# A fixed operation table for a whole attention-and-MLP kernel, in place of a scheduler and hand-written ends

## The chip, the cores and the metric

The kernel runs on one core of one Trainium2 chip. The metric is the device time of one execution in microseconds (us), so lower is better. Most executions of a kernel agree within about 1% here; an execution can fall in a slower state, and verdicts use the other ("fast") ones alone.

Names used below: PE is the tensor engine, DVE the vector engine, ACT the scalar engine, SP the queue that issues most loads. PSUM is the memory that PE writes; a *bank* is used here for 512 fp32 columns of it (the scores' tile in the program is 4 x 512). A *softmax block* is one tile of scores (128 x 2048) with its exponential; there are 68. S is "the score matmuls of a block". PEld in the profile is PE's loading of weights, POOL the fifth engine. An *F tile* is one of the 14 blocks of 128 hidden tokens. AV is "attention-value", the product p @ v. Line numbers such as L219 are those of a helper that records operations.

## The reference, cut to what matters

```python
h = layernorm(x) * (1 + ca) + sa            # x: 2048 x 512; sa, ca, ga, ... = silu(c) @ w_mod
q, k, v = split(h @ wqkv)                   # 32 heads of 16
p = softmax(where(0 <= i - j < 256, q k^T / 4, -1e9))
x = x + ga * ((p @ v) @ wo)
h = layernorm(x) * (1 + cb) + sb
u = gelu(layernorm(h)^T @ w1 + b1)          # a matmul over the 2048 rows; 1792 hidden tokens
x = x + gb * (u @ w2 + b2)^T
```

So there are a start (loads, first norm, first projections), a long middle (sliding-window attention, with the first half of the w1 products as filler), and a tail (last norm, the other half of w1, gelu, w2, stores). w1 contracts over rows: its products with the last rows need the last attention output.

## The kernel before: the parts that the argument touches

The loads are issued first, in the order written, on two queues:

```python
nc.scalar.dma_start(out=c4[:], ...)                                # ACT's queue
for v in (0, 1):
    nc.scalar.dma_start(out=wmod[:, :, v * D : (v + 1) * D], ...)  # 512 KB each
for t in range(4):
    dma.dma_start(out=xres[t][:], ...)                             # SP's queue: x, 128 KB a tile
# ... q, k, v weights, x 4..7, the rest of w_mod, wo, x 8..15 ...
dma.dma_start(out=b1b[:], in_=B_b1.rearrange("(j p) -> p j", p=P)) # last: b1 and b2, element by element
dma.dma_start(out=b2b[:], in_=B_b2.rearrange("(j p) -> p j", p=P))
```

The middle is a list of operations with costs and dependencies. A list scheduler in the program puts them in order before building. All score tiles live in the same four PSUM banks, so S of a block waits for the exponential of the block before:

```python
s = op(f"S{i}", "PE", 0.28, e_s, deps=[k_done[G, g8], q_done[G, g8], masks_built] + prev_exp, ...)
x = op(f"E{i}", "ACT", 1.78, e_e, deps=[s] + e_war, ...)
# in the scheduler: other work may not hold up the next S or the next exponential by more than
S_TOL = 0.1
E_TOL = 0.3
```

The tail is written by hand, after the scheduled part:

```python
def mlp1(fcs, scs):
    for sc in scs:                # rows outside, F tiles inside
        for fc in fcs:
            nc.tensor.matmul(ftiles[fc], lhsT=w1s(sc, fc), rhs=hb[sc][:], ...)
first = list(range(6))
mlp1(first, range(8, NT))         # hb[12..15] are the last norm's
for fc in first:
    gelu(fc)                      # addition, gelu, and a DVE multiplication by the gate
# ... the other 8 F tiles, then 16 output tiles of 14 matmuls each, finish(), store
```

The softmax here doesn't subtract the row's maximum and nothing guards it: scores larger than these inputs give would overflow.

## Time and profile before

321.87 us, median of 3 runs (320.91 to 322.01). The profiled execution has a span of 319.8 us. I cut it at the first and the last scores:

| stage | from, to (us) | length |
|---|---|---|
| start, to the first scores | 0, 17.44 | 17.4 |
| attention, first to last scores | 17.44, 217.43 | 200.0 |
| tail, from the last scores | 217.43, 319.8 | 102.4 |

The head of the profile page of before: span, then busy time and share of the span by engine, with the number of instructions.

```profile
span 319.8 us, 12671 instructions
PE 256.3 (80%) x5884; PEld 148.1 (46%) x5937; DVE 196.0 (61%) x376; ACT 176.5 (55%) x168; POOL 32.5 (10%) x87
```

No engine is full over the whole span: the limit differs by stage. The group of exponentials (busy time, mean ns, then ACT's idle time before them and who ended most of it) and that of the scores on PE show the alternation in the middle:

```profile
L219 ACT ACTIVATE et<-pss 128x2048 bf16<-128x2048 f32 x68 | 127.5, 1875 | 29.6 <-PE pss L219 20.3
L219 PE MATMUL pss<-QT,KT 32*64 32x32 bf16 (+5 forms) x1744 | 34.4, 209 | 22.7 <-ACT et L219 20.9
```

The timeline of before, start: first column the time, second the duration, then engine, operation, tiles; in brackets the idle time of that engine before it and what ended it. `ps_fm` makes the modulation vectors from `wmod`; `h1T` is the normed, transposed input of the projections; `KT` the keys as the scores need them; `pss` the scores.

```profile
7.06 0.59 PE L219 MATMUL ps_fm<-sT,wmod 128*128 128x1 bf16 x16 [0.84 <-DMA wmod<-in_w_mod_dram]
7.92 0.68 DVE L219 BATCH_NORM_STATS2 st<-x 128x6 f32<-128x512 bf16 x1
9.81 0.59 PE L219 MATMUL ps_fm<-sT,wmod 128*128 128x1 bf16 x16 [2.17 <-DMA wmod<-in_w_mod_dram]
...
11.80 1.90 DVE L219 TENSOR_SCALAR h1T<-pt,modFM 128x512 bf16<-128x512 bf16 x4 [0.81 <-PE pt L219]
15.97 1.41 DVE L219 TENSOR_SCALAR KT<-pk,mask_par 128x512 bf16<-128x512 f32 x2 [2.27 <-PE pk L219]
17.44 0.40 PE L219 MATMUL pss<-QT,KT 32*128 32x256 bf16 x8 [0.52 <-DVE KT L219]
```

The timeline of before, first part of the tail:

```profile
217.43 0.40 PE L219 MATMUL pss<-QT,KT 32*128 32x256 bf16 x8 [0.16 <-ACT et L219]
...
217.94 1.88 ACT L219 ACTIVATE et<-pss 128x2048 bf16<-128x2048 f32 x1
219.72 0.62 ACT L219 ACTIVATE lz<-lz 128x512 f32<-128x512 f32 x1
...
220.37 0.69 DVE L219 TENSOR_TENSOR OT<-pox,lz 128x512 bf16<-128x512 f32 x1 [2.37 <-ACT lz L219]
222.42 0.70 PE L219 MATMUL pox<-el,VT 128*32 128x32 bf16 x64
...
227.63 0.69 DVE L219 TENSOR_TENSOR x<-pa,x 128x512 bf16<-128x512 f32 x1 [0.50 <-PE pa L219]
...
242.93 1.38 DVE L219 TENSOR_SCALAR hb<-h,mv,rs 128x512 bf16<-128x512 bf16 x4 [0.60 <-ACT rs L219]
243.39 3.57 PE L950 MATMUL pu<-hb,w1p 128*128 128x512 bf16 x8 [9.01 <-DVE hb L219]
...
250.32 1.89 DVE L970 TENSOR_TENSOR a<-pu,part 128x512 f32<-128x512 f32 x3 [6.01 <-PE pu L950]
```

Read: last scores at 217.43, the last attention-value matmuls (`pox`) at +5.0, the first updated x of the last group at +10.2, the last `hb` (input of the MLP) complete at +26.9, first gelu addition 6.0 after that. PE waits 9.01 us for `hb`.

### The profile page before, as it was taken

What the parts mean: (1) busy time and instruction counts of PE and PEld (TensorE: products, weight loads), DVE (VectorE), ACT (ScalarE), POOL (GpSimd) and SP (SyncE); (2) the same over time, 40 slices, a digit from 0 to 9 for tenths busy, and PEclk for the clock granted to TensorE, in tenths of its full rate; (3) what the DMA queues carried; (4) which work ended last, traced back from release to release, by engine and by line L of the source; (5) the groups of instructions that cost most, each with busy time, mean ns of one, the idle gap of its engine ahead of it and who ended that gap; (6) DMA issues with size and microseconds to landing.
All of it is one profiled execution on the core that took longest, in us unless ns stands there. A gap on an engine that the chain in (4) does not pass through costs nothing.

```text
span 319.8 us, 12671 instructions
## 1 busy us (share of the span) xinstructions
PE 256.3 (80%) x5884; PEld 148.1 (46%) x5937; DVE 196.0 (61%) x376; ACT 176.5 (55%) x168; POOL 32.5 (10%) x87
## 2 busy tenths in 40 slices
PE   0678898867897778958888889787935899999973
PEld 0354466444574556624555554544412344444431
DVE  5574988448799746996521669531684667436433
ACT  1168897967887977777787776785102443000000
POOL 8102410130013410003001000000000000000000
PEclk9999999999999999989999999997985999999999
DMA  7993000790000000000201202122002990101100
GB/s 214 338 341 34 3 4 6 201 259 7 5 4 2 4 5 4 4 2 4 70 16 56 70 2 79 58 68 70 3 0 93 412 408 14 60 33 51 49 33 33
DMA packets 31453, 24.94 MB, mean 78 GB/s; under 512 B 6056, under 2 KB 29608, under 8 KB 31400
## 3 DMA queue, kind: packets, MB, share of 16 engines
q1 hardware_dynamic: 30336, 23.08, 23.6%
q10 hardware_dynamic: 1064, 1.05, 1.0%
q8 instruction: 46, 0.75, 0.9%
q14 instruction: 7, 0.06, 0.1%
HBM read 22.03 MB, written 2.10 MB: 75 GB/s over the span
## 4 chain that ended last, share of the span: by engine, by line
PE 46%; ACT 34%; DVE 14%; issue 4%; DMA 1%; POOL 0%; ACTq 0%; DVEq 0%
ACT et L219 30%; PE pu L1004 15%; PE pss L219 10%; PE pu L950 7%; PE pox L219 4%; DVE st L219 3%; PE poy L219 3%; PE pv L219 2%; DVE h L219 2%; PE pk L219 2%; DVE xn L219 1%; ACT rs L219 1%; PE pq L219 1%; ACT lz L219 1%; DVE o L987 1%
## 5 line engine op out<-in xcount | busy, mean ns | idle before, releaser
L219 ACT ACTIVATE et<-pss 128x2048 bf16<-128x2048 f32 x68 | 127.5, 1875 | 29.6 <-PE pss L219 20.3
L219 PE MATMUL pss<-QT,KT 32*64 32x32 bf16 (+5 forms) x1744 | 34.4, 209 | 22.7 <-ACT et L219 20.9
L1004 PE MATMUL pu<-guT,w2r 128*128 128x512 bf16 x220 | 49.3, 379 | 2.8 <-DVE o L987 2.5
L219 PEld LDWEIGHTS <-KT 32*64 32x64 bf16 (+1 forms) x1744 | 24.3, 97 | 39.2 <-issue 35.4
L586 POOL TENSOR_SCALAR KT<-kb,mask_par 128x512 bf16<-128x512 bf16 x30 | 24.5, 827 | 135.4 <-DVE kb L219 75.4
L950 PE MATMUL pu<-hb,w1p 128*128 128x512 bf16 x110 | 28.3, 410 | 11.6 <-DVE hb L219 9.0
L219 PEld LDWEIGHTS <-VT 128*32 128x32 bf16 x1680 | 29.0, 95 | 16.8 <-issue 13.8
L1004 PEld LDWEIGHTS <-w2r 128*128 128x128 bf16 x224 | 21.9, 98 | 29.6 <-issue 3.7
L219 PE MATMUL pox<-et,VT 128*32 128x224 bf16 (+3 forms) x720 | 33.7, 240 | 1.7 <-issue 1.5
L219 PE MATMUL poy<-et,ones_bd 128*32 128x224 bf16 (+3 forms) x720 | 33.0, 237 | 2.1 <-issue 2.1
L987 DVE SCALAR_TENSOR_TENSOR o<-bc_gb,b2FM,pu 128x512 f32<-128x512 bf16 x16 | 11.9, 747 | 25.0 <-PE pu L1004 25.0
L219 PE MATMUL pu<-hb,w1p 128*128 128x512 bf16 x95 | 24.8, 380 | 2.4 <-issue 2.2
L950 PEld LDWEIGHTS <-w1p 128*128 128x128 bf16 x112 | 11.6, 104 | 27.1 <-issue 16.1
L219 DVE COPY part<-pu 128x512 f32<-128x512 f32 x11 | 7.6, 690 | 25.0 <-PE pu L219 25.0
L219 PEld LDWEIGHTS <-ones_bd 128*32 128x32 bf16 x784 | 19.7, 96 | 6.5 <-issue 6.0
L219 DVE BATCH_NORM_STATS2 st<-x 128x6 f32<-128x512 bf16 x32 | 21.7, 679 | 0.2
L219 DVE TENSOR_TENSOR el<-et,maskl 128x2048 bf16<-128x2048 bf16 x16 | 20.0, 1264 | 1.4 <-ACT et L219 1.4
L219 PE MATMUL pq<-h1T,wqkv 128*128 128x512 bf16 x53 | 17.4, 414 | 2.0 <-issue 1.0
L219 DVE TENSOR_TENSOR OT<-pox,lz 128x512 bf16<-128x512 f32 x16 | 11.0, 685 | 12.2 <-ACT lz L219 12.2
L219 PE MATMUL pv<-wqkv,h1T 128*32 128x256 bf16 x512 | 17.1, 273 | 1.6 <-issue 1.6
L219 DVE TENSOR_SCALAR VT<-pv,par_of 128x512 bf16<-128x512 f32 x19 | 13.6, 745 | 7.2 <-PE pv L219 6.0
L219 PEld LDWEIGHTS <-wqkv 128*128 128x128 bf16 x128 | 11.0, 101 | 14.9 <-issue 5.8
(81 smaller groups left out, 306.0 us busy)
## 6 DMA issues: line engine op xcount, KB each, us to landing
w1p<-in_B_w_dram SPq DMA_DIRECT2D x14, 512.0 KB, 4.0
w2r<-in_B_w_dram SPq DMA_DIRECT2D x14, 512.0 KB, 9.3
x<-in_A_x_dram SPq DMA_DIRECT2D x16, 128.0 KB, 5.2
wmod<-in_w_mod_dram SPq DMA_DIRECT2D x4, 512.0 KB, 6.9
out_dram<-otile SPq DMA_DIRECT2D x16, 128.0 KB, 1.7
wmod<-in_w_mod_dram ACTq DMA_DIRECT2D x2, 512.0 KB, 6.2
wqkv<-in_A_wqkv_dram SPq DMA_DIRECT2D x2, 384.0 KB, 7.2
wqkv<-in_A_wqkv_dram SPq DMA_DIRECT2D x1, 512.0 KB, 7.9
```

Of the source, the lines that this page charges most:

```text
L219: ins = call(*args, **kwargs)
L586: eng.tensor_scalar(out=KT[r3][g8][:, :, :, par, :], in0=src[:].rearrange("p (b s k) -> p b s k", s=2, k=HB), scalar1=mask_par[:, par : pa ...
L950: nc.tensor.matmul(ftiles[fc], lhsT=w1s(sc, fc), rhs=hb[sc][:], start=(sc == 8), stop=(sc == NT - 1), skip_group_check=True,)
L987: nc.vector.scalar_tensor_tensor(out=o1[:], in0=bc_gb[:], scalar=b2FM[:, tb : tb + 1], in1=py, op0=ALU.mult, op1=ALU.add,)
L1004: nc.tensor.matmul(ftiles[100 + t], lhsT=w2r[:, fc, t * P : (t + 1) * P], rhs=guT[fc][:], start=(fc == 0), stop=(fc == NF - 1), skip_group ...
```

## The change

Intent: one set of some 1090 numbered operations for everything (loads, attention, both MLP matmuls, stores), cut finer than before, emitted in the order of a table that was searched beforehand, instead of a scheduler for the middle and hand-written ends. The core of the diff (cut):

```diff
-def run_schedule(ops, rings, log=None):      # the list scheduler, about 90 lines
+ORDER = """
+41 30 0 3 42 55 5 49 4 48 13 38 12 54 56 29 1 40 57 78 6 58 2 34 8 37 25 ...
+... 93 19 92A 91D 94 31 24 96D 95A 17 97 98 100 99A 101 104 102A 103D ...
+"""                                          # A or D: on ACT or on DVE
+def run_order(ops):
+    for word in ORDER.split():
+        o = ops[int(word.rstrip("AD"))]
+        o.emit(engines[word[-1]] if word[-1] in engines else next(iter(o.engs)))
+WARM = 24                                    # zero matmuls while PE waits for the first loads
@@ loads become operations of the table @@
-    dma.dma_start(out=b2b[:], ...)           # last
+    o_b = [load("b1", ...), load("b2", ...)] # words 29 and 30
@@ the first transposed input may be copied by either engine @@
-            h = op("h1T", "DVE", 0.95, e_h, deps=[a, o_fm] + before, pos=p_tr)
+                frees.append(op("h1T", {"DVE": 0.45, "ACT": 0.6}, e_h, deps=[tr[1], o_fm] + before, ...))
@@ the tail becomes operations too, F tile by F tile @@
-    mlp1(first, range(8, NT))
+            for lo in range(8, NT, 2):       # two matmuls an operation, in the order of the table
@@ the gate is applied to the result, not to the hidden activations @@
-        nc.vector.tensor_tensor(out=guT[fc][:], in0=g[:], in1=bc_gb[:], op=ALU.mult)
-            in0=bc_gb[:], scalar=b2FM[...], in1=py, op0=ALU.mult, op1=ALU.add
+            in0=ftiles[100 + tb], scalar=b2FM[...], in1=bc_gb[:], op0=ALU.add, op1=ALU.mult
```

In the first words, 0 is c; 1 and 2 the two halves of `wmod`; 3, 4, 5, 6 the first four x tiles; 7 to 28 the other loads (12 and 13 are x tiles of the next group); 29 and 30 are b1 and b2. So b2 now leads SP's queue.

## The prediction

> **What bounds the kernel now** (timeline and chain of waits; span 319.8 us):
> 1. Start: first scores at 17.4 us, after load, statistics, xn, transposes, four h1T copies (1.9 us on DVE), q, k, two KT copies (1.4 us on DVE). The first q and k matmuls are 0.43 us apart, later ones 0.216[...].
> 2. Attention: 17.4 to 217.4 us (last scores), 68 softmax blocks. All score tiles share four PSUM banks, so exponential (1.88 us) and scores (0.53 with hand-over; long form 1.25) alternate: floor 2.44 us, 3.16 for the eight long ones. PE does the rest between. I summed PE's program order between successive scores at measured spacings (512 columns 0.216 us, V projection 0.87, window AV 0.43, local AV 0.73, 0.09 per change of array tiling) and took the larger of sum and floor: 193 us, against 200.0 measured. Some periods are overloaded (up to 7.2 us), others have 1.3 us of work.
> 3. Tail: 102.4 us. The last group's norm chain is serial on DVE (first x at 227.6, last hb about 244); PE waits 9.0 us for hb[...], waits again for the first gelu additions (250.3), then runs back to back; 4.4 us drain.
>
> **What changes.** The matmuls are the same, plus 24 zero ones at the start. It removes 14 DVE multiplies of guT by bc_gb (0.42 us, mostly hidden), splits projections into halves, gives ACT half of the first h1T and KT copies, splits the rs of the first and last group, and fixes the order of everything.
>
> **Costs.**
> - Start: copies shared by ACT and DVE save 0.8 + 0.7 us[...]. Against it: the wmod loads on ACT's queue now follow the exponential that waits for c (3.8 us instead of 1.4), and b2b and b1b lead the SP queue, 3840 two-byte packets that kept the DMA busy about 2.6 us near 25 us. Estimate: first scores at 16.5 us (15.5 to 18.5).
> - Attention: the same count over the new order gives 184 us (largest period 3.6): work is spread evenly. With before's excess of 3.7%, 191.5 (186 to 198), a gain of 8.5. Sixteen partial matmuls (3.5 us) moved into the tail.
> - Tail, from the last scores: AV is no longer held behind w1 matmuls, so the first x comes at about +5.6 us instead of +10.2; the DVE chain still takes 15.8, so hb is complete near +22 instead of +26.6. Meanwhile PE does Wo and half the rows of eight F tiles. Then 288 matmuls remain (62 us) instead of 312, gelu additions follow at once[...], 4.4 drain: +91. Gain 11.5.
>
> Sum: 16.5 + 191.5 + 91 = 299 us span; measured times are some 2 us above the span: **300.5 us**, 8 in 10 between 292 and 310. All of it is on the critical path. Faster by over 2%: 0.94; within 2%: 0.05; slower by over 2%: 0.01.
>
> **What would show it.** First scores at 15.5 to 18.5; first to last scores 186 to 198 us, PE's waits for exponentials and ACT's for scores both smaller; first x of the last group within 7 us of the last scores; PE's wait for hb below 6 us; first gelu addition within 2 us of the last hb; then back-to-back matmuls and the same drain.
>
> **What would make it wrong.** A late x tile, with DVE in order, would hold the first groups: the fixed order may ignore real load arrival. Finer in-order pieces could wait on each other more than 3.7%. [...]

The sum: 16.5 + 191.5 + 91 = 299 us of span, 300.5 us of time. That PE is slower after standing idle, that zero matmuls prevent this, and that a busier PE loses clock was the author's assumption, which no trace shows. Two of these are in the sum: up to 1.3 us of gain in the start's 16.5 (about what six matmuls at 0.43 instead of 0.216 us come to), and 2 us for PE's restart in the tail's +91 (22 + 62 + 2 + 4.4 = 90.4). What the trace of before shows is the spacing: 0.43 us for the first q and k matmuls; and after the 9.01 us wait for `hb` the first eight matmuls took 3.57 us, 0.45 each, at a granted clock of 0.50 (237.1 to 247.3 us), where later ones come every 0.216 us.

## The result, and the profile after

308.87 us median (307.76 to 310.87, 4 runs) against 321.39 of before (4 runs). The ratio is 0.963, 95% interval 0.956 to 0.970: faster. A ratio here is the mean time of one kernel's fast runs over the mean of the other's fast runs of the same rounds, so it is not quite the ratio of the medians quoted.

The time fell inside the range, but only 12.5 us of the forecast 21. By stage, from the two timelines:

| | before | after | forecast for after |
|---|---|---|---|
| first scores at | 17.4 | 21.6 | 16.5 |
| first to last scores | 200.0 | 190.7 | 191.5 |
| last scores to the end | 102.4 | 93.7 | 91 |
| span | 319.8 | 306.0 | 299 |

The attention is as forecast, the tail misses by 2.7 us, and the start **lost** 4.1 us where 0.9 was to be gained. Most of the miss is in the first 22 us. The head of the page of after:

```profile
span 306.0 us, 12754 instructions
PE 263.4 (86%) x5961; PEld 148.4 (49%) x5961; DVE 190.9 (62%) x367; ACT 178.3 (58%) x178; POOL 29.3 (10%) x87
```

The same two groups as before, exponentials and scores:

```profile
L169 ACT ACTIVATE et<-pss 128x2048 bf16<-128x2048 f32 x68 | 127.6, 1876 | 33.3 <-PE pss L169 31.7
L169 PE MATMUL pss<-QT,KT 32*64 32x32 bf16 (+5 forms) x1744 | 35.4, 210 | 14.1 <-ACT et L169 10.1
```

PE's waits for exponentials halved (20.9 to 10.1 us), but ACT's waits for scores grew (20.3 to 31.7).

The timeline of after, start:

```profile
0.81 0.43 SPq L169 DMA_DIRECT2D b2b<-in_B_b_dram  x1
...
4.57 1.47 ACTq L169 DMA_DIRECT2D wmod<-in_w_mod_dram  x2
...
12.65 0.69 DVE L169 BATCH_NORM_STATS2 st<-x 128x6 f32<-128x512 bf16 x1 [5.28 <-DMA x<-in_A_x_dram]
13.78 0.15 DVE L169 COPY sT<-st_ps 128x4 bf16<-128x4 bf16 x1
13.98 0.99 PE L169 MATMUL ps_fm<-sT,wmod 128*128 128x1 bf16 x32 [5.80 <-DVE sT L169]
...
15.89 0.78 ACT L169 ACTIVATE h1T<-pt,modFM 128x512 bf16<-128x512 bf16 x1 [1.76 <-PE pt L169]
16.70 0.99 DVE L169 TENSOR_SCALAR h1T<-pt,modFM 128x512 bf16<-128x512 bf16 x2 [1.46 <-ACT h1T L169]
17.73 0.78 ACT L169 ACTIVATE h1T<-pt,modFM 128x512 bf16<-128x512 bf16 x1 [1.06 <-DVE h1T L169]
...
21.58 0.40 PE L169 MATMUL pss<-QT,KT 32*128 32x256 bf16 x8 [0.58 <-DVE KT L169]
```

DVE waits 5.28 us for the fourth x tile (12.65; before 7.92). DVE works in order, as the small copy `sT` shows, which the modulation needs and which has nothing to do with x: PE had written its input by 6.8, but it starts at 13.78, behind those statistics, and PE's modulation matmuls with it (13.98; before complete from 9.81). And the four h1T copies, shared by two engines to save time, take turns: 15.89 to 18.51 is 2.6 us, against 1.90 on DVE alone before.

The timeline of after, first part of the tail:

```profile
209.23 0.59 ACT L169 ACTIVATE lz<-poy 128x512 f32<-128x512 f32 x1
...
209.85 0.63 ACT L169 ACTIVATE lz<-lz 128x512 f32<-128x512 f32 x1
...
210.51 0.69 DVE L169 TENSOR_TENSOR OT<-pox,lz 128x512 bf16<-128x512 f32 x1 [0.68 <-ACT lz L169]
...
212.30 0.40 PE L169 MATMUL pss<-QT,KT 32*128 32x256 bf16 x8
...
212.91 0.67 PE L169 MATMUL pox<-el,VT 128*32 128x32 bf16 x64
...
218.31 0.69 DVE L169 TENSOR_TENSOR x<-pa,x 128x512 bf16<-128x512 f32 x1 [0.17 <-PE pa L169]
...
233.64 0.41 DVE L169 TENSOR_SCALAR hb<-h,mv,rs 128x512 bf16<-128x512 bf16 x1 [0.30 <-ACT rs L169]
235.43 0.69 DVE L169 TENSOR_TENSOR a<-pu,part 128x512 f32<-128x512 f32 x1 [1.38 <-PE pu L169]
```

From the last scores (212.30): attention-value matmuls at +0.6 (before +5.0), first x at +6.0 (+10.2), last `hb` complete at +21.7 (+26.9), first gelu addition 1.4 after that (6.0). From the last `hb` to the end it is 72.0 us (75.5). So the tail's 8.7 us are 4.4 from the earlier attention-value matmuls, 1.0 from the norm chain, 3.5 after `hb`, less 0.2 between.

Last, PE of after has stalls that no wait explains ("issue": the engine waited for nothing that the profile shows). The three longest of the attention, from the timeline:

```profile
74.49 0.27 PE L169 MATMUL pox<-et,VT 128*32 128x224 bf16 x2 [1.72 <-issue]
...
177.64 0.22 PE L169 MATMUL poy<-et,ones_bd 128*32 128x96 bf16 x2 [1.49 <-issue]
...
203.48 0.22 PE L169 MATMUL poy<-et,ones_bd 128*32 128x96 bf16 x2 [2.31 <-issue]
```

All such stalls over 0.45 us between 18 and 222 us sum to 9.7 us (before: 5.25). I had not expected them.

### The profile page after: what moved, and what is told of

It reads as the page before. It is cut to its first block, busy times and chain, and to the rows that moved or that the text cites. A ratio compares the mean times of both kernels' runs of the same rounds, so it can differ in the third digit from the quotient of the medians.

```text
span 306.0 us, 12754 instructions
## 1 busy us (share of the span) xinstructions
PE 263.4 (86%) x5961; PEld 148.4 (49%) x5961; DVE 190.9 (62%) x367; ACT 178.3 (58%) x178; POOL 29.3 (10%) x87
## 4 chain that ended last, share of the span: by engine, by line
PE 66%; ACT 20%; issue 5%; DVE 4%; DMA 3%; SPq 1%; ACTq 0%; DVEq 0%
PE pu L169 32%; ACT et L169 18%; PE pss L169 12%; PE pq L169 7%; PE pox L169 5%; PE poy L169 4%; PE pa L169 3%; DMA x<-in_A_x_dram 3%; PE pv L169 2%; SPq L169 1%; DVE o L169 1%; DVE a L169 1%; PE pt L169 1%; ACT h1T L169 1%; PE ps_b L169 1%
## 5 line engine op out<-in xcount | busy, mean ns | idle before, releaser
L169 ACT ACTIVATE et<-pss 128x2048 bf16<-128x2048 f32 x68 | 127.6, 1876 | 33.3 <-PE pss L169 31.7
L169 PE MATMUL pu<-guT,w 128*128 128x512 bf16 x224 | 50.0, 379 | 2.5 <-DVE o L169 2.5
L169 PE MATMUL pss<-QT,KT 32*64 32x32 bf16 (+5 forms) x1744 | 35.4, 210 | 14.1 <-ACT et L169 10.1
L169 POOL TENSOR_SCALAR KT<-kb,mask_par 128x512 bf16<-128x512 bf16 x30 | 21.6, 736 | 153.4 <-DVE kb L169 80.9
L169 PEld LDWEIGHTS <-w 128*128 128x128 bf16 x224 | 21.9, 98 | 29.5 <-issue 3.6
L169 PE MATMUL poy<-et,ones_bd 128*32 128x224 bf16 (+3 forms) x720 | 31.7, 237 | 4.8 <-issue 4.8
L169 PE MATMUL pq<-h1T,wqkv 128*128 128x512 bf16 x128 | 34.9, 393 | 0.9 <-ACT h1T L169 0.3
L169 PE MATMUL pox<-et,VT 128*32 128x224 bf16 (+3 forms) x720 | 32.2, 239 | 2.6 <-issue 1.9
L169 PEld LDWEIGHTS <-w1p 128*128 128x128 bf16 x224 | 20.4, 98 | 27.1 <-issue 5.2
L169 DVE SCALAR_TENSOR_TENSOR o<-pu,b2FM,bc_gb 128x512 f32<-128x512 f32 x16 | 11.9, 748 | 28.0 <-PE pu L169 27.9
L169 DVE BATCH_NORM_STATS2 st<-x 128x6 f32<-128x512 bf16 x32 | 21.7, 678 | 6.2 <-DMA x<-in_A_x_dram 6.1
L169 DVE TENSOR_SCALAR VT<-pv,par_of 128x512 bf16<-128x512 f32 x27 | 18.9, 738 | 9.7 <-PE pv L169 9.7
L169 DVE TENSOR_TENSOR OT<-pox,lz 128x512 bf16<-128x512 f32 x16 | 11.0, 687 | 14.9 <-ACT lz L169 10.6
L169 ACT ACTIVATE rs<-mv,eps_t 128x4 f32<-128x4 f32 (+2 forms) x19 | 5.6, 292 | 22.1 <-DVE mv L169 22.1
L169 PE MATMUL pa<-wod,OT 128*128 128x512 bf16 x64 | 17.4, 388 | 1.1 <-DVE OT L169 0.6
L169 PEld LDWEIGHTS <-wqkv 128*128 128x128 bf16 x128 | 10.5, 100 | 13.1 <-issue 5.1
```

Source lines behind the costliest of these rows:

```text
L169: ins = call(*args, **kwargs)
```

## The experiments

Twelve kernels ran, each beside runs of before on the same chip. All results were correct except one. Edits are shown against the changed kernel ("changed") or the kernel before ("before").

### The start: which loads are in the wrong place?

Theory: two things at once hold the start of the changed kernel. (1) The fourth x tile is late, behind b2, b1 and later tiles. (2) `wmod` is late: it is issued at 4.57 instead of 1.44 and meets the two-byte packets of b1 and b2. Rival: it is only the place of the x tile.

**a_bias_last**: changed, b1 and b2 after the other start loads.

```diff
+ORDER = moved(["29", "30"], "23")   # these words, to right after word 23
```

> The changed kernel with only its two bias loads (b1b, b2b: 3840 packets of 2 bytes) moved behind all other start loads. In the changed kernel the fourth x tile's statistics start at 12.65 us and the first scores at 21.6. Theory 1 (the two-byte packets on the SP queue[...] hold up the fourth x tile): statistics of that tile start by 8.5 us, first scores at 16.5 to 18, whole kernel 3.5 to 5 us faster than the changed kernel, about 304 to 305. Theory 2 (two tiles of the next group and the shuffled tile order ahead of it hold it up): statistics not before 11 us, total within 1 us of the changed kernel. Theory 3 (wmod issued late on ACT's queue): first scores stay above 20 us.

308.63 us, ratio to before 0.958 (0.952 to 0.964). The fourth x tile came at 8.30, but the second half of `wmod` only let its matmuls start at 12.96; first scores at 20.1 instead of 21.6.

**a_x3_first**: changed, the fourth x tile right after the second.

```diff
+ORDER = moved(["6"], "4")
```

> The changed kernel with only the load of the fourth x tile moved ahead of two tiles of the next group and of b1b; b2b still leads. Theory 1: the statistics of the fourth tile start by 7.5 us, but the first q and k weights still stand behind b1b and come at about 12 us, so first scores at 17.5 to 19, 2 to 4 us gained. Theory 2: the same tile early, first scores at 16.5 to 17.5, the whole loss back. Theory 3: first scores above 20 us.

309.73 us, ratio 0.962 (0.955 to 0.968). x was early (last statistics of the four at 7.71), and the last modulation matmuls at 13.18: first scores at 21.26. The rival falls: the x tile alone gains 0.3 us. The line that shows the second limit, first in a_bias_last:

```profile
12.96 0.55 PE L177 MATMUL ps_fm<-sT,wmod 128*128 128x1 bf16 x16 [2.79 <-DMA wmod<-in_w_mod_dram]
```

and in a_x3_first:

```profile
13.18 0.59 PE L177 MATMUL ps_fm<-sT,wmod 128*128 128x1 bf16 x16 [2.04 <-DMA wmod<-in_w_mod_dram]
```

One half of (2) is not borne out: in a_bias_last no bias packets were on the way, and the second `wmod` load still landed at 12.92, not before the 12.42 of after. That `wmod` is late does not hang on meeting those packets.

**a_wmod_first**: changed, the two `wmod` loads right after c.

```diff
+ORDER = moved(["1", "2"], "0")
```

> The changed kernel with only the two wmod loads moved ahead of the exponential of c on ACT. Theory 3 (wmod late): first scores at 19 us or earlier, at least 2 us gained. Theory 1: [...]the x tiles come no earlier: fourth tile's statistics at 11 to 13.5 us, first scores at 20.5 to 22.5, total within 1.5 us.

308.66 us, ratio 0.958 (0.951 to 0.965). Now x was late (11.13) and the modulation at 12.46; first scores at 20.97. The totals of these three runs are not told apart from the 308.87 of the change.

**b_bias_first**: the reverse, in the kernel before: only b2 and b1 put at the head of SP's queue.

```diff
+dma.dma_start(out=b2b[:], ...)
+dma.dma_start(out=b1b[:], ...)
 for t in range(4):
     dma.dma_start(out=xres[t][:], ...)
...
-dma.dma_start(out=b1b[:], ...)
-dma.dma_start(out=b2b[:], ...)
```

> The kernel before with only its two bias loads moved to the head of the SP queue. Theory 1: the x tiles wait for 3840 two-byte packets[...]; first scores from 17.4 to 20 to 22 us, total 2.5 to 4.5 us slower than before. Theories 2 and 3 (tile order or late wmod, neither of which is here): first scores at most 18.5, total within 1 us of before.

325.99 us, ratio 1.010 (1.001 to 1.020). First scores moved from 17.4 to 21.4: two loads of 4 KB, element by element, cost 4 us when they stand first. The first x statistics began at 9.31 instead of 4.97 and the modulation ended 3.7 us later.

How the two queues share the DMA engines: from 7 to 9 us of after, with b1 on SP's queue and `wmod` on ACT's, the DMA engines took 698 packets of SP's queue, with hardly any data (1.4 KB), among 599 of ACT's with 0.60 MB; a packet took 9 and 48 ns in the mean, and in order of start 46% of the neighbours are of different queues. The fourth x tile, issued behind b1, landed at 12.63, after b1 (11.85). In b_bias_first the second `wmod` load came late too (its modulation matmuls from 9.81 to 13.51), but it was also issued late (7.43 instead of 3.03), so that delay does not show by itself that one queue holds up the other. In the profiled run of after, the DMA engines were 0.85 busy at 3 GB/s between 2 and 3 us, with b2 ahead of the x tiles on its queue and `wmod` not yet issued (before in the same microsecond: 0.81 busy, 245 GB/s).

**a_loads_old**: changed, all 31 loads first in the order of before.

```diff
+LOADS = [str(n) for n in range(31)]
+ORDER = " ".join(LOADS + [w for w in ORDER.split() if w not in LOADS])
```

> The changed kernel with all 31 start loads issued first, in the order of the kernel before (x tiles 0 to 3 first, biases last, wmod ahead of the exponential of c). The first batch showed that either repair alone (biases last: first scores 20.1 us; wmod first: 21.0) leaves the other limit standing. Theory 1+3 (both must be repaired): the four statistics start at about 5 to 8 us, modulation product ends by 10.6, h1T still costs 2.6 us on two engines, first scores at 16.5 to 17.7 us, total 3 to 5 us below the changed kernel, 304 to 306. Rival (whatever is won before the first scores is lost again in the first blocks, where V projections and later loads limit): first scores early, but the sixth exponential not before 34.5 us (36.9 in the changed kernel) and the total within 1.5 us of it.

303.63 us (302.58 to 304.43), ratio 0.942 (0.936 to 0.948). The interval lies wholly below that of the change (0.956 to 0.970), each against before of its own session. This is the lowest median. From its timeline:

```profile
8.74 0.94 PE L172 MATMUL ps_fm<-sT,wmod 128*128 128x1 bf16 x32 [0.43 <-DVE sT L172]
...
16.89 0.40 PE L172 MATMUL pss<-QT,KT 32*128 32x256 bf16 x8 [0.58 <-DVE KT L172]
```

First scores at 16.9, 4.7 us earlier than after and inside the forecast's 15.5 to 18.5. Each single repair had gained 0.3 to 1.5 us of the first scores, because the other load then set the pace: the theory of two joint limits holds. Two bounds: this run restores the place of all 31 loads, so that moving x and `wmod` alone would do as much is not shown; and in its profile first to last scores took 192.3 us against 190.7, so 1.6 of the 4.7 us were given back there.

**a_start**: a_loads_old, and the h1T copies dealt so that each engine keeps one PSUM bank.

```diff
-... 93 19 92A 91D 94 31 24 96D 95A
+... 93 19 92D 91D 94 31 24 96A 95A
```

> As a_loads_old, and in addition the four first h1T copies dealt out by PSUM bank: DVE takes both copies of one transposed tile, ACT both of the other, instead of one of each. Theory (two engines on the same PSUM bank are made to take turns, so the split saved nothing): first to last h1T shrinks from 2.6 to 1.2 to 1.7 us and first scores come 0.8 to 1.4 us earlier than in a_loads_old. Rival (they take turns because both write h1T, or because ACT is simply slow): 2.3 us or more stay.

From its timeline:

```profile
10.33 0.99 DVE L172 TENSOR_SCALAR h1T<-pt,modFM 128x512 bf16<-128x512 bf16 x2 [0.24 <-PE pt L172]
10.81 1.45 ACT L172 ACTIVATE h1T<-pt,modFM 128x512 bf16<-128x512 bf16 x2 [1.92 <-PE pt L172]
```

Now the two engines overlap: 10.33 to 12.26, 1.93 us instead of 2.6. But that is what DVE needed alone before (1.90), and the first scores gained only 0.3 (16.57); both sizes that I had expected were missed. The total, 304.24 us (303.88 to 305.42), ratio 0.945 (0.939 to 0.952), is not told apart from a_loads_old's. So the shared copies of the change saved nothing, where the prediction had put 0.8 + 0.7 us on them. What the traces show is this: two engines reading one transposed tile took turns (2.6 us), two engines reading different ones overlapped (1.93). (Each transposed tile fills one bank, so the runs do not tell bank from tile; that both write h1T is not the reason, since they still did in a_start.)

### The attention: what do the stalls without a cause cost, and what are they?

**a_no_w1_second**: changed, five of the seven second-half w1 loads left out (the first half's data is used again: the result is wrong).

```diff
+        if half == 1 and pair < 5:
+            w1t[pair, 1] = w1t[pair, 0]
+            return
```

> The changed kernel without the five loads of w1's second half that run during attention (it reuses the first half: a wrong result on purpose). In the changed kernel PE stands still 1.49 and 2.31 us, labelled issue, in the middle of an AV group at 177.6 and 203.5 us while these loads run; all such stalls lie at the same place in every 256 instructions. Theory (PE waits there for its next instructions, and their fetch is slowed by data loads): both shrink to 1.0 us or less, first to last exponential 2 to 3 us shorter than the 190.7 to 193.4 of the same order with loads. Rival (the stalls have nothing to do with the loads): they stay at 1.3 to 2.4 us.

306.72 us (4 runs: 302.83 and 305.86 fast, 307.99 and 307.59 slow), ratio of the fast ones 0.945 (0.935 to 0.955). The stall at 177.6 was gone (under 0.45 us), that at 203.5 shrank from 2.31 to 1.59, that at 74.5, where first-half loads still ran, stayed (1.98). In the six profiles of this table with all loads, these two were 1.3 to 1.7 and 2.0 to 2.9 us. So the loads lengthen these two stalls. What this is worth in time is not settled: the interval of the two fast runs lies below that of the change, but the profiled run was a slow one and its attention took 190.9 us, no less than after's.

**a_shift**: a_loads_old, with 63 small zero matmuls more at the start, where PE idles.

```diff
-        te.matmul(box["warm"][:], lhsT=zt[:, 0:P], rhs=zt[:], start=True, stop=True)
+        for q in range(4) if box["n"] <= 21 else [None]:   # a quarter of the columns each
+            te.matmul(box["warm"][:, cols], lhsT=zt[:, 0:P], rhs=zt[:, cols], ...)
```

> The changed kernel with the old load order, and with 21 of its 24 zero matmuls at the start each cut into four of a quarter of the columns: 63 matmuls (126 tensor instructions with their weight loads) more, at a place where the tensor engine idles. Theory (the long stalls without a visible cause are fetches of the next block of instructions, tied to the place in the program): every such stall moves to an instruction about 126 earlier in the kernel's own order, so that its number, counted in the longer program, is again near 192 in 256; none of the stalls at 68.6, 108.6, 172.7 and 198.8 us of the version without the cut stays at its matmul. Rival (they belong to the work at these places, a buffer, a semaphore or a load): the stalls stay before the same matmuls. In both cases first scores at 16.5 to 17.2 us and the total within 3 us of that version's 303.6.

305.86 us (303.79 to 307.59), ratio 0.950 (0.944 to 0.956); first scores at 15.85, earlier than expected (in this profile the clock was not halved at the start; see "Start, the zero matmuls" below). Two stalls from its timeline:

```profile
71.04 0.59 PE L172 MATMUL pa<-wod,OT 128*128 128x512 bf16 x1 [2.68 <-issue]
...
172.22 0.27 PE L172 MATMUL poy<-et,ones_bd 128*32 128x224 bf16 x1 [1.98 <-issue]
```

I numbered PE's matmuls in the trace and counted two instructions for each (its weight load and itself). In the changed kernel, a_loads_old and a_shift **every** one of the 24 stalls over 0.45 us stands before an instruction whose number is 190 modulo 256, in a_shift counted with the 126 new ones. In a_loads_old the stalls near 68.6, 108.6, 172.7 and 198.8 stood at the numbers 3262, 5566, 9150 and 10430. In a_shift number 9150 belongs to another matmul, and the stall is there (172.22). At 68.6, 108.6 and 198.8 no stall over 0.45 us was left. A place in the program, not the work there, makes a stall possible.

The packed trace also holds the packets of the instruction queue; in order, they pair with these places from the second on. In these three profiles, at each of the 24 stalls the packet of that place had ended 1.1 to 1.7 us before PE went on. At the 99 such places without any stall it had mostly ended earlier, 2.7 to 3.1 us before in the median of each profile. So PE stood still where its next block of instructions came late.

The size of a block fits the period of 256: the page of after shows 46 packets and 0.75 MB on the instruction queue, 16 KB each, and 11922 matmuls and weight loads of PE, 259 for each packet. From 71 to 76 us of after, around the 1.72 us stall, the DMA engines were 0.94 busy at 246 GB/s. In the twelve profiles counted, the stalls over 0.45 us between 18 and 222 us sum to 4.2 us (b_fmajor_av) to 13.8 us (b_spread_fill), and the longest is 3.18 us (b_spread_fill).

**b_spread**: the kernel before, with two settings of its scheduler changed so that the filler work spreads as evenly as the table's.

```diff
-S_TOL = 0.1
+S_TOL = 0.4
-            p_late = [start_of(G) - 1.5 + k * 1.0 for k in range(6)]
+            p_late = [start_of(G) - 4.0 + k * 1.0 for k in range(6)]
```

> The kernel before with two numbers of its scheduler changed: PE work may delay the next scores by 0.4 us instead of 0.1, and the late q and k projections may come 2.5 blocks earlier. My count over PE's order falls from 193 to 183.6 us, the changed kernel's is 184.4; the longest period from 7.2 to 4.8. Theory (attention was won by spreading PE's work evenly, and nothing else of the change matters there): first to last exponential from 200.0 to 189 to 194 us, total 6 to 10 us below before. Rival (it was won by finer pieces, by copies moved off ACT and by better known costs): attention stays at 196 us or more, total within 4 us of before.

319.93 us (319.05 to 320.68), ratio 0.993 (0.987 to 0.999). By count this order is nearly as good as the table's, but from first to last exponential it took 202.3 us (before 200.0, after 190.7). My theory, that the count alone decides, fell. The profile shows stalls of 10.7 us in all (before 5.25), one of 3.11, and a lower clock. These are its windows (length; busy time of PE, PEld, DVE, ACT, POOL; granted clock; DMA share; GB/s) around that stall. A packet counts in the window in which it starts, so the DMA share can pass 1:

```profile
45.00:50.00 5.00, 2.28 (x125) 2.14 (x118) 0.75 (x1) 3.03 (x3) 1.18 (x2) 1.00 1.21 292
50.00:55.00 5.00, 4.03 (x128) 2.10 (x128) 2.20 (x4) 2.40 (x2) 0.00 (x0) 0.73 1.15 284
55.00:60.00 5.00, 3.89 (x59) 2.17 (x62) 3.30 (x6) 3.10 (x3) 0.00 (x0) 0.59 0.09 21
```

The loads are at their peak, PE stalls (its busy time falls to 2.28 of 5 us), then the clock is halved for 6.8 us. That the stall causes the dip is not shown: of the five dips in this attention, two began during a stall or within 2 us after one. The clock records of before, after and b_spread show the dips as half clock for 3.413 us or two or three times that (the last one is cut by the end of the run).

In counting again (PE's program order at measured spacings) I found an error of mine: the prediction's floor of 3.16 us for a block with scores in 32-column pieces does not hold for the sixteen or so blocks that have such pieces beside others; 2.44 does. The corrected counts are 185.2 (before), 176.0 (after) and 177.6 (b_spread), not 193 and 184. The difference was right (9.2), so the forecast of the attention came out right.

**b_spread_fill**: b_spread with zero matmuls in underloaded blocks, to hold the clock (that it falls when PE idles was my assumption).

```diff
+    for a, b in zip(starts, starts[1:]):
+        idle = (3.16 if order[a][1].engs["PE"] == 0.5 else 2.44) - work   # estimate per block
+        if idle > 0.8:
+            fills[a] = int((idle - 0.25) / 0.216)
```

> The spread version of the kernel before, with some 40 zero matmuls added after the scores of those blocks in which the tensor engine would idle for more than 0.8 us. Theory (the spread version lost what its even order saved to a throttled clock[...]): the mean granted clock rises from 0.946-0.957 to at least 0.965 and the time from first to last exponential falls from 202.3 to 193 to 198 us. Rival (it lost it to the waits for instructions alone, or to hand-overs that the sum leaves out): clock up or not, this time stays at 200 us or more.

332.41 us (330.11 to 333.69), ratio 1.032 (1.025 to 1.040): slower. Clock 0.938 to 0.952, no higher; first to last exponential 212.8 us. The theory as I put it fell. Nor is the rival shown, since the edit did not raise the clock. Stalls summed to 13.8 us, and five of the six dips of the attention began during such a stall or within 0.2 us of its end. The zero matmuls neither prevent the stalls nor run for free: by the corrected count they add 4.6 us (182.2), the longer stalls 3.1; the last 2.8 of the 10.5 us are open.

### The tail: what made it shorter?

**b_fmajor_av**: the kernel before, with the last attention-value and output matmuls kept ahead of those of w1, and the last rows' w1 matmuls F tile by F tile.

```diff
-                nc.tensor.matmul(                # in mlp1
+                te.matmul(                       # kept in program order while pinned
...
-    mlp1(first, range(8, NT))
+    pinned[0] = True
+    mlp1(first, range(8, 12))
+    pinned[0] = False
+    for fc in first:
+        mlp1([fc], range(12, NT))
```

> The kernel before with one part of the new order alone: in the tail the last group's attention-value matmuls and its output projections are kept ahead of the first-MLP matmuls that wait for the last norm, and those go tile by tile for the last four row blocks. Theory (the tail's gain comes from the attention-value matmul no longer standing behind matmuls that wait): first x of the last group about 6 us after the last scores instead of 10.2, last hb some 4 us earlier, first gelu addition within 2 us of the last hb instead of 6, time from the last exponential to the end 94 to 97 us instead of 101.9, attention unchanged (199 to 202), the total 5 to 8 us less. Rival (the gain comes from the finer pieces and the split norm, or from the missing multiplication by the gate): the tail stays above 100 us.

321.65 us (320.63 to 323.67), ratio 1.000 (0.994 to 1.006): nothing gained. (The profiled execution had a granted clock of 0.95 almost throughout; the reading below is of order and waits.) From its timeline:

```profile
218.82 1.88 ACT L219 ACTIVATE et<-pss 128x2048 bf16<-128x2048 f32 x1
220.59 0.62 ACT L219 ACTIVATE lz<-lz 128x512 f32<-128x512 f32 x1
221.25 0.69 DVE L219 TENSOR_TENSOR OT<-pox,lz 128x512 bf16<-128x512 f32 x1 [2.34 <-ACT lz L219]
...
221.99 0.70 PE L219 MATMUL pox<-el,VT 128*32 128x32 bf16 x64 [2.80 <-DVE OT L219]
...
227.97 0.69 DVE L219 TENSOR_TENSOR x<-pa,x 128x512 bf16<-128x512 f32 x1 [0.48 <-PE pa L219]
```

Here no w1 matmul stands before the attention-value matmuls, and they still come 3.7 us after the last scores (218.31): they wait 2.80 us for `OT`, which frees their PSUM bank, and `OT` waits for the second `lz`, which stands on ACT behind the last exponential. In before it is the same chain, 219.72 to 220.37. In after both `lz` run ahead of the last two exponentials (209.23 and 209.85), so the bank is free before the last scores. My reason for the earlier x, "AV is no longer held behind w1 matmuls", was the smaller part: in before, six w1 matmuls did stand between the end of `OT` (221.06) and the attention-value matmuls (222.42), 1.4 of the 4.4 us, but with them out of the way the first x came at +9.7 instead of +10.2. That the forecast of +5.6 (measured +6.0) was near is luck. What the table does is finish the unit before one exponential earlier, and let its two short ACT steps go first; in before they were split around the last exponential. No run changed ACT's order alone, so this rests on the waits in the traces. First gelu addition was still 5.2 us after the last `hb`: PE restarted at 0.43 us a matmul after waiting 5.24 us, and the addition waited for PE until 249.82, though its own F tile has only four of these matmuls. The sixteenth began at 249.33: I take it that the addition waits for all four F tiles of one PSUM tile; that is argued, not shown.

**b_no_gu**: the kernel before without the gate multiplications.

```diff
-        nc.vector.tensor_tensor(out=guT[fc][:], in0=g[:], in1=bc_gb[:], op=ALU.mult)
-            out=o1[:], in0=bc_gb[:], scalar=..., in1=py, op0=ALU.mult, op1=ALU.add
+            out=o1[:], in0=py, scalar=..., in1=bc_gb[:], op0=ALU.add, op1=ALU.mult
```

> The kernel before with only the arithmetic part of the change: the 14 multiplications of the hidden activations by the gate are gone and the gate is applied to the result instead. Theory (hidden behind the matmuls, as the prediction said): the total within 1 us of before, at most 1.5 us less. Rival (they hold up the first matmuls of the second MLP and are a good part of the tail's 8.7 us): 3 us or more less.

322.56 us median of 6 (317.15 to 324.9), before 321.71 (319.52 to 324.73). One run, 317.15, counts as fast; the other five lie more than 1.5% above it. The profiled one, itself slow, has 75.2 us from the last `hb` to the end, against 75.5 in before. As far as one profile tells, the multiplications were hidden.

## Why the prediction was right or wrong, point by point

- **Total**: 300.5 forecast, 308.87 measured; inside 292 to 310, and faster by over 2% as said. The error of the span is +5.1 (start), -0.8 (attention), +2.7 (tail).
- **Start: the step that failed.** "Estimate: first scores at 16.5 us (15.5 to 18.5)"; measured 21.58. The prediction had seen that "b2b and b1b lead the SP queue", and even named "A late x tile, with DVE in order" as what could go wrong, but its own terms leave only 0.6 to 1.9 us for the late loads (17.4 less 0.8, 0.7 and the term of up to 1.3 is 14.6 to 15.9). They cost 4.7 us (21.58 against 16.89 with the old load order). In its place the runs showed two joint limits, the fourth x tile (12.65) and `wmod` (second half 12.96 to 13.18 once x was early). With the old load order alone the total came to 303.63. That the total still fell inside its range, with the start outside its own, is owed to the width of the range.
- **Start, the copies: wrong in mechanism.** "copies shared by ACT and DVE save 0.8 + 0.7 us": they save nothing; on h1T because the engines take turns at one transposed tile (2.6 us against 1.90), and the two KT copies took 1.47 us against 1.41.
- **Start, the zero matmuls: not got.** Up to 1.3 us was counted on. In after the granted clock is 0.50 from 11.3 to 18.1 us, over the first two of its eight q and k matmuls. In a_loads_old it is 0.50 from 11.5 to 14.9, and the last six took 2.46 us; in a_shift it is 1.00 there, they took 1.46, and the first scores came 1.0 us earlier. This is one profile of each; no run tested it by itself, so what sets the clock there is not shown.
- **Attention: right in size.** 191.5 forecast, 190.7 measured. Of the two signs named, PE's waits for exponentials fell (20.9 to 10.1), but ACT's for scores rose (20.3 to 31.7). The absolute count was wrong (above) and its difference right. What of the table won these 9.3 us is not shown: b_spread, with nearly as good a count, won nothing in the attention; its longer stalls (10.7 us) and lower clock (0.946) stand beside that, but no run separated them.
- **Tail: right in most sizes, wrong in one reason.** First x +6.0 (forecast 5.6), last `hb` +21.7 (22), PE's wait for the last `hb` none (below 6; its two waits for `hb`, 0.8 us together, are at 142 us), gelu addition 1.4 after (within 2). The early x is for the most part ACT's order, by the waits, and not w1 matmuls. The term mis-sized was the end: from the last `hb`, 288 matmuls remained, as forecast (62.2 us at 0.216), but gaps between them were 4.9 us where the prediction had 2. The time from the start of the last one was 4.8 (sum 71.9; 72.0 measured); from its end, as the prediction counted, 4.4 as forecast.
- **The clock**: PE was busier in after (86% of the span, before 80%), and its granted clock was 0.981 (before 0.972).

## What to carry to other kernels

A searched order is only as good as the loads it assumes. Before trusting a fixed table, read in the trace when each load of the first 10 us lands, and keep element-by-element loads out of that time (two of them, 3840 packets of two bytes, cost 4 us in b_bias_first); where two loads are late, repairing one can show little (0.3 to 1.5 us here, against 4.7), so undo them together. Before a short operation is moved or shared, ask what it frees and which PSUM tile it reads: PE waited 2.8 us for an accumulator that a 0.6 us step behind the last exponential held, and four copies shared by two engines took 2.6 us where one engine took 1.90. When PE stalls for "issue", number its instructions, and look when the packets of the instruction queue ended: here a period of 256, each time just after such a packet, meant that PE waited for its program, and two of three such waits shrank (1.49 to under 0.45, 2.31 to 1.59) when later loads were left out.
